# Stores of converted weights and of bias groups issued by GpSimd instead of the sync engine

## The chip, the cores and the metric

The kernel runs on one core of one Trainium2 chip. Its time is the device time of one execution in microseconds (us); the kernel before took 1183.42 us in the median of three runs (1183.03 to 1185.1). The engines are named as the profile names them: PE is TensorE, DVE is VectorE, ACT is ScalarE, POOL is GpSimd, SP is the sync engine. "PEld" is the loading of weights into TensorE, "SPq" and "DVEq" are the instruction queues of an engine. A DMA is a transfer between the chip's memory (HBM) and the core's on-chip memory (SBUF); it is started by an instruction of SP or another engine and moved by the core's 16 DMA engines.

## The reference

Attention with a learned bias, then two gated feed-forward blocks, all in float32. Cut to what matters:

```python
# B, H, S, D = 4, 8, 576, 64
psi_rel = np.log1p(np.abs(rel)); psi_i = np.log1p(np.maximum(pos[:, None], 1.0))
x = (psi_rel / psi_i)[..., None]
h = np.maximum(x @ w1 + b1, 0.0)                 # 32 hidden values for each pair (i, j)
bias = h @ w2                                    # one value for each head and pair
scores = (q @ k^T) / np.sqrt(D) + bias.transpose(2, 0, 1)[None]
attn = exp(scores - max); attn = attn / (sum(attn) + 1e-9)
x = (attn @ v), heads laid side by side: 2304 tokens x 512
x = (sigmoid(x @ w_gate) * (x @ w_val)) @ w_out                      # d_ff 1536
h = x @ w_in;  out = (h * clip(h + 3, 0, 6) / 6) @ w_out2            # d_ff 2048
```

The weights of the feed-forward blocks are handed over as float64; the bias does not depend on the batch.

## The kernel before, in words

The 576 query positions are cut into five chunks (128, 128, 128, 128 and 64 positions for all four batches). A chunk goes through attention first, in 16 units (4 pairs of heads times 4 batches; 8 units for the last chunk), and then through 68 feed-forward steps (`STEPS`, line 51), each a product of a 512 x 128 block of weights with up to 512 tokens. `moe_step` (line 430) runs one step; `product` (line 403) makes each product of three passes, high part times high part, high times low, low times high, so 12 matmuls of 512 columns a step.

The program has a lead and five blocks. The lead (lines 481 to 523) makes the bias of the first chunk and its attention. Block k (lines 622 to 634) runs the 68 steps of chunk k and, between them, the bias and the attention of a later chunk.

**The bias.** It is made in groups of 16 positions, 36 in all. `bias_hidden` (line 117) makes the hidden values `z` on ACT and DVE, `bias_mm` (line 130) multiplies by the second weight matrix on PE, `bias_out` (line 140) brings the group from PSUM to the tile `bo` (three buffers, line 72) on DVE or ACT (lines 147 and 149) and stores it to `biasD[c]` in HBM, 288 KB a group (line 153). `bias_read` (line 161) loads the stored bias of two heads as `bm`, 576 KB. Groups 0 to 7 are the first chunk's; the lead also makes groups 8 to 10.

**The weights.** In block 0 only, `w_load` loads a step's weights as float64 bits (`wd`, 512 KB, line 370; three buffers), and `w_split` (lines 376 to 398) turns them into two float32r parts in `wp` (six buffers): ACT makes `cm` (line 385), DVE works on it three times (lines 386, 387, 390), ACT writes the high part (line 395), DVE the low part (line 396). The result is used by the step's product and stored to `wsp` in HBM, 512 KB (line 397). From block 1 on a step loads its `wp` from `wsp` (line 374).

**The order.** In the lead the order on PE, ACT, DVE and SP is that of the source (line 484). After it the order of PE alone is written out; a scheduler puts DVE, ACT, SP and POOL in an order by its own estimate of times. Every engine runs its instructions in order, and a DMA-issuing instruction holds its queue until what it waits for is there. All transfers are issued by SP; POOL only sets four constants.

The lines around the two stores:

```python
        i0 = 16 * G - QC[c][0]
        nc.sync.dma_start(out=biasD[c][i0:i0 + 16].rearrange("i h j -> (i h) j"), in_=bo)      # L153
...
        nc.scalar.activation(out=wv[:, 0], in_=f, func=AF.Copy)                                # L395
        nc.vector.tensor_tensor(out=wv[:, 1], in0=f, in1=wv[:, 0].bitcast(F32), op=ALU.subtract)
        nc.sync.dma_start(out=wsp[n], in_=wv.bitcast(F32))                                     # L397
```

Of the kernel before, what the change touches and what calls it, by code (L numbers as in the profile page):

```python
# [9 lines left out]
F32 = mybir.dt.float32  # L10
# [46 lines left out]
def fused_kernel(ctx: ExitStack, tc: tile.TileContext, qd, kd, vd, tz, rd, zc, w2b, iden, wpack, out):  # L57
    nc = tc.nc
# [27 lines left out]
    biasD = [dr_p.tile([n, H, S], F32, name=f"biasD{c}") for c, (_, n) in enumerate(QC)]  # L86
    wsp = dr_p.tile([NSTEP, 128, 2, 512], F32, name="wsp")
# [17 lines left out]
    for g in (2, 3):  # L105
        nc.tensor.matmul(
            out=ps[32 * g:32 * g + 32, 0:2], lhsT=w2b_t, rhs=zc_t[:, 0:2], start=True, stop=True,
# [32 lines left out]
    def bias_out(G):  # L140

        ps = bo_q.pop(G)
        c = min(G // 8, NC - 1)
        bo = bo_p.tile([128, S], F32, name="bo")
        bv = bo.rearrange("p (a j) -> p a j", a=2)
        if c == 1:
            nc.scalar.activation(out=bv, in_=ps[:, :, 0:NI], func=AF.Identity, scale=D ** 0.5, bias=cv_t)
        else:
            nc.vector.tensor_scalar(
                out=bv, in0=ps[:, :, 0:NI], scalar1=D ** 0.5, scalar2=cv_t, op0=ALU.mult, op1=ALU.add  # L150
            )
        i0 = 16 * G - QC[c][0]
        nc.sync.dma_start(out=biasD[c][i0:i0 + 16].rearrange("i h j -> (i h) j"), in_=bo)  # L153

# [220 lines left out]
    def w_split(n):  # L377

        if n >= NSTEP:
            return  # L380
        wd = wf_q.pop(n)
        low, high = wd[:, :, 0], wd[:, :, 1]
        m = A["cv"].tile([128, 512], U32, name="cm")
        f = m.bitcast(F32)
        nc.scalar.activation(out=f, in_=high.bitcast(F32), func=AF.Copy, scale=2.0 ** -112)  # L385
        nc.vector.tensor_scalar(out=m, in0=m, scalar1=3, scalar2=None, op0=ALU.logical_shift_left)
        nc.vector.scalar_tensor_tensor(  # L387
            out=m, in0=low, scalar=29, in1=m, op0=ALU.logical_shift_right, op1=ALU.bitwise_or
        )
        nc.vector.scalar_tensor_tensor(  # L390
            out=m, in0=high, scalar=0x80000000, in1=m, op0=ALU.bitwise_and, op1=ALU.bitwise_or
        )
        wp = w_p.tile([128, 2, 4, 128], F32R, name="wp")
        wv = wp.rearrange("p s c m -> p s (c m)")
        nc.scalar.activation(out=wv[:, 0], in_=f, func=AF.Copy)  # L395
        nc.vector.tensor_tensor(out=wv[:, 1], in0=f, in1=wv[:, 0].bitcast(F32), op=ALU.subtract)  # L396
        nc.sync.dma_start(out=wsp[n], in_=wv.bitcast(F32))  # L397
        wq[n] = wp


# [80 lines left out]
    with ExitStack() as lead:  # L481
# [9 lines left out]
        for G in range(NG0 + NG1 + 1):  # L491
            if G < NG0 + NG1:
                for g in range(4):
                    bias_hidden(G, g)
                bias_mm(G)
            if G:
                bias_out(G - 1)
            if G == NG0:
                bias_read(us[0])
# [3 lines left out]
        for n in range(NL + 2):  # L503
            if n + 3 < NL:
                att_load(us[n + 3])
            if n < NL:
                att_exp(us[n])
            if n + 1 < NL:
                att_min(us[n + 1])
            if 1 <= n <= NL:  # L510
                for part in range(3):
                    att_tr(us[n - 1], part, mm_ps)
            if n < NL:
                att_norm(us[n])
            if n >= 2:
                att_av(us[n - 2], mm_ps)
                att_x(us[n - 2])
            if n + 2 < NL:
                att_qk(us[n + 2])
            if n >= NL:  # L520
                w_split(n - NL)
            if n == NL - 4:
                gate = issued[0]
# [13 lines left out]
    def chunk_bias(c, t0, dt, done=0):  # L537

        i0, n = QC[c]
        G0, nG = i0 // 16 + done, n // 16 - done  # L540
        ev = []
        for g in range(nG):
            ev.append((t0 + dt * g, lambda G=G0 + g: [bias_hidden(G, t) for t in range(4)]))
        for g in range(0, nG, 2):
            def outs(G=G0 + g, two=min(2, nG - g)):
                for i in range(two):
                    bias_mm(G + i)
                for i in range(two):
                    bias_out(G + i)
            ev.append((t0 + dt * g + dt + 1, outs))  # L550
        return ev
# [69 lines left out]
    with tc.manual_schedule(engines={ET.PE}):  # L621
        for k in range(NC):
            if k == 1:
                conv.close()
                A.update(ks=late("ks", 2), qs=late("qs", 2))
            ev = block_events(k)
            for i in range(NSTEP):
                while ev and ev[0][0] <= i:
                    ev.pop(0)[1]()
                w_load(k * NSTEP + i + WA)  # L630
                w_split(k * NSTEP + i + WB)
                moe_step(k, i, P, mm_ps)
            for e in ev:
                e[1]()
# [64 lines left out]
```

## Time and profile before

| what | value |
|---|---|
| median of three runs | 1183.42 us (1183.03 to 1185.1) |
| profiled execution: time, span of its profile | 1183.61 us, 1181.8 us |
| PE busy | 1157.1 us (98%) |
| DVE, ACT busy | 641.1 us (54%), 563.9 us (48%) |
| POOL busy | 0.2 us |
| mean DMA rate | 252 GB/s, one queue |
| bias stores, stores of converted weights | 36 of 288 KB, 68 of 512 KB |

The 1.8 us between the time and the span lie outside what the profile shows. An engine's busy time is the union of its instructions; PE's ends are modelled, so a busy PE is not PE at its peak. In the list of transfers "us to landing" is the time from the issue to the arrival of all data. In the chain of waits each piece is what held the end of the program at that time.

### The profile page before, as it was taken

The page shows a single profiled execution, that of the slowest core. Times are in us where ns is not written, and L with a number is a line of the kernel's source. Part 1 is how long each engine was busy: PE and PEld are TensorE (multiplying, and loading weights), DVE is VectorE, ACT ScalarE, POOL GpSimd, SP SyncE. Part 2 cuts the span into 40 slices and gives each one's busy share as a digit, 9 for nine tenths or more (in the row PEclk, how much of TensorE's full clock was granted, in tenths as well). Part 3 has the DMA queues.
Part 4 walks back from the last instruction along what each step waited for, and adds up shares of the span by engine and source line. Part 5 has one row for each costly group of instructions (what it writes and reads, how often), then busy time and mean ns, then how long its engine had stood idle before and what let it go on. Part 6 is the DMA issues. An engine that isn't in the chain of part 4 may idle for free.

```text
span 1181.8 us, 20334 instructions
## 1 busy us (share of the span) xinstructions
PE 1157.1 (98%) x7676; PEld 928.3 (79%) x7676; DVE 641.1 (54%) x1524; ACT 563.9 (48%) x1133; POOL 0.2 (0%) x4
## 2 busy tenths in 40 slices
PE   7998989999999999999999999999999999999998
PEld 3676767777777787777888787888878778789998
DVE  6787988999973544585534543453432315331232
ACT  7776766677752434575534543454322214331231
POOL 0000000000000000000000000000000000000000
PEclk9899999999999999999999999999999999999999
DMA  6886899999987676566575656565685857567997
GB/s 217 283 281 215 306 340 353 368 353 321 380 271 239 209 231 223 196 223 214 207 245 190 228 187 219 196 205 190 197 268 194 261 190 238 192 194 249 361 366 273
DMA packets 115264, 297.65 MB, mean 252 GB/s; under 512 B 20448, under 2 KB 35168, under 8 KB 115168
## 3 DMA queue, kind: packets, MB, share of 16 engines
q1 hardware_dynamic: 115168, 296.36, 73.1%
q8 instruction: 61, 1.00, 0.3%
q14 instruction: 35, 0.29, 0.1%
HBM read 245.32 MB, written 50.99 MB: 251 GB/s over the span
## 4 chain that ended last, share of the span: by engine, by line
PE 87%; DMA 5%; DVE 5%; ACT 2%; issue 1%; SPq 0%; ACTq 0%; DVEq 0%
PE ps L412 66%; PE ps L279 6%; PE ps L260 6%; DMA wd<-wpack 3%; PE ps L320 3%; PE ps L135 3%; PE ps L212 2%; DMA biasD<-bo 1%; DVE cm L390 1%; DVE cm L387 1%; PE ps L326 1%; DVE wp L396 1%; ACT s L237 1%; DVE s L227 1%; ACT cm L385 0%
## 5 line engine op out<-in xcount | busy, mean ns | idle before, releaser
L412 PE MATMUL ps<-xyh,wp 128*128 128x512 f32 (+1 forms) x1600 | 479.2, 375 | 6.9 <-ACT wp L395 3.5
L412 PEld LDWEIGHTS ps<-xyh,wp 128*128 128x128 f32 x1600 | 290.9, 189 | 70.7 <-issue 7.2
L412 PE MATMUL ps<-gh,wp 128*128 128x512 f32 (+1 forms) x1120 | 343.7, 378 | 0.0
L412 PE MATMUL ps<-xyl,wp 128*128 128x512 f32 (+1 forms) x800 | 295.9, 370 | 0.7 <-DVE xyl L425 0.7
L412 PEld LDWEIGHTS ps<-gh,wp 128*128 128x128 f32 x1120 | 203.5, 189 | 40.9 <-issue 6.4
L412 PE MATMUL ps<-gl,wp 128*128 128x512 f32 (+1 forms) x560 | 206.8, 369 | 0.0
L412 PEld LDWEIGHTS ps<-xyl,wp 128*128 128x128 f32 x800 | 151.5, 189 | 23.7 <-DVE xyl L425 1.1
L263 ACT ACTIVATE pT<-ps 128x384 f32<-128x384 f32 x216 | 100.6, 488 | 125.3 <-PE ps L260 124.7
L421 ACT ACTIVATE gh<-tmp 128x512 fp32r<-128x512 f32 (+1 forms) x140 | 82.4, 589 | 111.6 <-DVE tmp L443 73.7
L423 DVE TENSOR_TENSOR gl<-tmp,gh 128x512 fp32r<-128x512 f32 (+1 forms) x140 | 89.0, 636 | 65.1 <-ACT gh L421 65.1
L237 ACT ACTIVATE s<-s,m 128x576 f32<-128x576 f32 x144 | 110.4, 769 | 25.6 <-DVE m L342 13.4
L412 PEld LDWEIGHTS ps<-gl,wp 128*128 128x128 f32 x560 | 105.9, 189 | 14.9
L260 PE MATMUL ps<-id_t,s 128*128 128x128 f32 x648 | 101.1, 277 | 0.9 <-ACT s L237 0.4
L260 PEld LDWEIGHTS ps<-id_t,s 128*128 128x128 f32 x648 | 79.0, 141 | 29.0 <-issue 5.9
L443 DVE SCALAR_TENSOR_TENSOR tmp<-tmp,ps 128x512 f32<-128x512 f32 (+1 forms) x60 | 38.0, 633 | 115.2 <-PE ps L412 115.2
L279 PE MATMUL ps<-pT,vt 128*64 128x128 f32 (+1 forms) x1600 | 90.9, 266 | 0.3 <-DVE xyl L299 0.3
L279 PEld LDWEIGHTS ps<-pT,vt 128*64 128x64 f32 x1600 | 78.9, 137 | 15.0 <-issue 11.0
L449 DVE SCALAR_TENSOR_TENSOR tmp<-tmp,ps 128x512 f32<-128x512 f32 (+1 forms) x80 | 50.5, 631 | 70.4 <-ACT tmp L448 68.8
L247 DVE TENSOR_SCALAR s<-s,r 128x576 f32<-128x576 f32 x144 | 68.2, 516 | 1.6
L439 ACT ACTIVATE tmp<-ps 128x512 f32<-128x512 f32 (+1 forms) x60 | 33.3, 554 | 73.6 <-PE ps L412 73.6
L448 ACT ACTIVATE tmp<-ps 128x512 f32<-128x512 f32 (+1 forms) x80 | 44.1, 551 | 46.8 <-PE ps L412 46.0
L299 DVE TENSOR_TENSOR xyl<-ps,xyh 128x128 fp32r<-128x128 f32 (+1 forms) x52 | 17.7, 340 | 87.2 <-ACT xyh L298 87.1
(50 smaller groups left out, 939.5 us busy)
## 6 DMA issues: line engine op xcount, KB each, us to landing
wp<-wsp SPq DMA_DIRECT2D x272, 512.0 KB, 4.0
wd<-wpack SPq DMA_DIRECT2D x68, 512.0 KB, 5.5
wsp<-wp SPq DMA_DIRECT2D x68, 512.0 KB, 4.9
vt<-vd SPq DMA_DIRECT2D x80, 320.0 KB, 4.5
kt<-kd SPq DMA_DIRECT2D x80, 288.0 KB, 5.1
biasD<-bo SPq DMA_DIRECT2D x36, 288.0 KB, 2.8
bm<-biasD SPq DMA_DIRECT2D x16, 576.0 KB, 5.0
qt<-qd SPq DMA_DIRECT2D x16, 256.0 KB, 6.4
```

The lines of the kernel that those rows point to most:

```text
L135: nc.tensor.matmul(out=ps[32 * g:32 * g + 32, j, 0:NI], lhsT=w2b_t, rhs=z[:, g, NI * j:NI * j + NI], start=True, stop=True, tile_position= ...
L237: nc.scalar.activation(out=s[:, h], in_=s[:, h], func=AF.Exp, scale=-1.0, bias=d["m"][:, h:h + 1], accum_out=r[:, h:h + 1],)
L247: nc.vector.tensor_scalar(out=s[:, h], in0=s[:, h], scalar1=r[:, h:h + 1], scalar2=None, op0=ALU.mult)
L260: nc.tensor.transpose(out=ps[:, t * NQ:t * NQ + NQ], in_=p[:, 128 * k:128 * k + 128], identity=id_t)
L263: nc.scalar.activation(out=d["pt"][:, 3 * part:3 * part + 3], in_=ps[:, 0:3 * NQ].rearrange("p (t n) -> p t n", t=3), func=AF.Copy,)
L279: nc.tensor.matmul(out=po[64 * h:64 * h + 64, n * a:n * a + n], lhsT=vt[:, v], rhs=pt[:, k, n * a:n * a + n], start=(t == 0), stop=(t == 4 ...
L412: nc.tensor.matmul(out=ps[:, 0:nt], lhsT=w[:, c, :], rhs=x[:, 0:nt], start=(first and c == 0 and i == 0), stop=(last and c == 3 and i == 2),)
L421: nc.scalar.activation(out=hi[:, 0:nt], in_=src, func=AF.Copy, scale=scale)
L423: nc.vector.tensor_tensor(out=lo[:, 0:nt], in0=src, in1=hi[:, 0:nt].bitcast(F32), op=ALU.subtract)
L443: nc.vector.scalar_tensor_tensor(out=th, in0=th, scalar=1.0, in1=ps, op0=ALU.add, op1=ALU.mult)
L448: nc.scalar.activation(out=t, in_=ps, func=AF.Relu, bias=3.0)
L449: nc.vector.scalar_tensor_tensor(out=t, in0=t, scalar=6.0, in1=ps, op0=ALU.min, op1=ALU.mult)
```

## The change

Both stores are issued by GpSimd's queue. Every load, and the stores of the output, stay with SP.

```diff
@@ bias_out
         i0 = 16 * G - QC[c][0]
-        nc.sync.dma_start(out=biasD[c][i0:i0 + 16].rearrange("i h j -> (i h) j"), in_=bo)
+        nc.gpsimd.dma_start(out=biasD[c][i0:i0 + 16].rearrange("i h j -> (i h) j"), in_=bo)
@@ w_split
         nc.vector.tensor_tensor(out=wv[:, 1], in0=f, in1=wv[:, 0].bitcast(F32), op=ALU.subtract)
-        nc.sync.dma_start(out=wsp[n], in_=wv.bitcast(F32))
+        nc.gpsimd.dma_start(out=wsp[n], in_=wv.bitcast(F32))
         wq[n] = wp
```

SP's list of the lead before, from the last load of the start on (the first eight bias stores are like the two shown):

```order
L490 DMA tz_t_96<-tz 128x448
L153 DMA biasD0_90<-bo_178 128x576
...
L153 DMA biasD0_90<-bo_297 128x576
L167 DMA bm_300<-biasD0_90 128x1152
L153 DMA biasD1_91<-bo_316 128x576
...
L153 DMA biasD1_91<-bo_336 128x576
L182 DMA kt_356<-kd 128x576
```

SP's list of the same place now, and below it POOL's list of the whole lead:

```order
L490 DMA tz_t_96<-tz 128x448
L167 DMA bm_300<-biasD0_90 128x1152
L182 DMA kt_356<-kd 128x576
L185 DMA vt_358<-vd 128x640
L167 DMA bm_377<-biasD0_90 128x1152
```

```order
L694 UNCONDITIONAL_BRANCH
L153 DMA biasD0_90<-bo_178 128x576
...
L153 DMA biasD0_90<-bo_297 128x576
L153 DMA biasD1_91<-bo_316 128x576
...
L153 DMA biasD1_91<-bo_336 128x576
L397 DMA wsp_95<-wp_1139 128x1024
```

The eleven stores of the lead left SP for POOL and kept their order among themselves; the load of `bm` now waits for stores of another queue.

In block 0, DVE's list before, around the first attention unit of the second chunk (`L227` adds the bias and takes the minimum, `L386`, `L387`, `L390` and `L396` convert weights, `wd_1650` is the load of one step, `wp_1712` its result):

```order
L387 SCALAR_TENSOR_TENSOR cm_1707<-wd_1650,cm_1707 128x512
L386 TENSOR_SCALAR cm_1757<-cm_1757 128x512
L390 SCALAR_TENSOR_TENSOR cm_1707<-wd_1650,cm_1707 128x512
L227 ISA s_1744,m_1745<-ps_1738,bm_1642 128x576
...
L423 TENSOR_TENSOR gl_1731<-tmp_1703,gh_1730 128x512
L387 SCALAR_TENSOR_TENSOR cm_1757<-wd_1679,cm_1757 128x512
L227 ISA s_1744,m_1745<-ps_1739,bm_1642 128x576
...
L396 TENSOR_TENSOR wp_1712<-cm_1707,wp_1712 128x512
```

The same place of DVE's list now:

```order
L387 SCALAR_TENSOR_TENSOR cm_1707<-wd_1650,cm_1707 128x512
L227 ISA s_1744,m_1745<-ps_1738,bm_1642 128x576
...
L423 TENSOR_TENSOR gl_1731<-tmp_1703,gh_1730 128x512
L227 ISA s_1744,m_1745<-ps_1739,bm_1642 128x576
...
L390 SCALAR_TENSOR_TENSOR cm_1707<-wd_1650,cm_1707 128x512
L386 TENSOR_SCALAR cm_1757<-cm_1757 128x512
...
L387 SCALAR_TENSOR_TENSOR cm_1757<-wd_1679,cm_1757 128x512
...
L390 SCALAR_TENSOR_TENSOR cm_1757<-wd_1679,cm_1757 128x512
L247 TENSOR_SCALAR s_1744<-s_1744,r_1746 128x576 x2
L396 TENSOR_TENSOR wp_1712<-cm_1707,wp_1712 128x512
```

The conversion of `wp_1712` now has the unit's softmax (`L227` to `L247`) and most of the next conversion ahead of its last step. PE's list is the same in both programs.

## Rows read from the trace of the kernel before

**Rows 1.** Busy time by stretch; columns: stretch, length, engines, TensorE clock, DMA share, GB/s.

```profile
99.25:237.72 138.47, 133.28 (x732) 100.86 (x732) 126.25 (x254) 92.67 (x174) 0.00 (x0) 0.99 0.92 334
237.72:1181.80 944.08, 939.77 (x6172) 770.55 (x6172) 444.11 (x1080) 397.50 (x800) 0.00 (x0) 1.00 0.71 241
```

**Rows 2.** What PE waited for from 238 us to the end.

```profile
PE ps L412 <- DVE xyl L425: 0.7, 1, 0.7
```

**Rows 3.** The chain of waits in the lead: start, length, what.

```profile
12.92 5.09 DMA biasD<-bo
...
19.97 3.23 DMA biasD<-bo
...
25.14 2.07 DMA biasD<-bo
...
27.35 4.59 DMA bm<-biasD
...
32.09 0.76 DVE s L227
```

**Rows 4.** Order of time in the lead on SP: start, length, what.

```profile
10.55 0.33 SPq L490 DMA_DIRECT2D tz_t<-tz  x1
11.45 14.00 SPq L153 DMA_DIRECT2D biasD<-bo  x8
```

**Rows 5.** The first bias store, alone in its window; then the DMA rate from 10 to 18 us.

```profile
DMA to landing us min/median/max: 5.9/5.9/5.9
...
GB/s 397 402 392 439 394 422 389 420 405 416 402 415 396 376 394 402 393 393 408 405 396 393 416 422 389 387 421 402 384 410 421 288 161 81 69 58 46 58 23 23
```

**Rows 6.** Order of time in the lead on DVE; in brackets idle time before, and its releaser.

```profile
14.52 1.06 DVE L126 TENSOR_SCALAR z<-tz_t,sc_t,zc_t 128x576 f32<-128x576 f32 x2
17.42 0.82 DVE L149 TENSOR_SCALAR bo<-ps,cv_t 128x576 f32<-128x576 f32 x1 [1.85 <-DMA biasD<-bo]
...
24.30 0.81 DVE L149 TENSOR_SCALAR bo<-ps,cv_t 128x576 f32<-128x576 f32 x1
25.03 2.04 DVE L126 TENSOR_SCALAR z<-tz_t,sc_t,zc_t 128x576 f32<-128x576 f32 x4
```

**Rows 7.** Order of time in the lead on PE.

```profile
7.24 9.55 PE L135 MATMUL ps<-z,w2b_t 128*32 128x288 f32 x80 [1.73 <-ACT z L124]
18.39 10.72 PE L135 MATMUL ps<-z,w2b_t 128*32 128x288 f32 x96 [1.60 <-DVE bo L149]
...
30.71 1.23 PE L212 MATMUL ps<-kt,qt 64*128 64x288 f32 x6 [0.92 <-ACT bo L147]
```

**Rows 8.** What SP's queue waited for, 99 to 238 us: total, times, longest.

```profile
SPq L370 <- DVE cm L390: 30.5, 25, 2.8
```

**Rows 9.** The chain of waits in block 0: the first and last of five loads.

```profile
145.17 8.14 DMA wd<-wpack
...
196.28 8.51 DMA wd<-wpack
```

**Rows 10.** PE in block 0: the costliest group, then two of its gaps in order of time.

```profile
L412 PE MATMUL ps<-xyh,wp 128*128 128x512 f32 x199 | 66.4, 405 | 6.9 <-ACT wp L395 3.5 <-DVE wp L396 3.4
...
99.25 0.50 PE L412 MATMUL ps<-xyh,wp 128*128 128x512 f32 x1 [2.43 <-ACT wp L395]
141.48 0.73 PE L412 MATMUL ps<-xyh,wp 128*128 128x512 f32 x2 [0.81 <-DVE wp L396]
```

**Rows 11.** Waits of ACT for loaded weights, 99 to 238 us.

```profile
ACT cm L385 <- DMA wd<-wpack: 9.6, 8, 2.8
```

**Rows 12.** Stores of `wp` in 99.25 to 237.72 us: issues, then landing.

```profile
L397 SPq DMA_DIRECT2D wsp<-wp x40: 319/326/1152, 99.9 to 236.5; - x40
...
DMA to landing us min/median/max: 2.6/5.3/10.0
```

**Rows 13.** Two DVE pieces of the chain in block 0.

```profile
169.44 0.60 DVE cm L387
...
171.63 0.93 DVE s L247 x2
```

## The prediction

> **What bounds the kernel now.** I read the busy time by stretch first [rows 1]. From 237.72 us to the end PE is busy 939.77 of 944.08 us and waits in all 0.7 us for another engine [rows 2]; whatever the change does, it can only be paid or earned in the 238 us before. There are two stages there. One is the lead, up to 99.25 us, which the chain below explains. In the other, the first part of block 0 (99.25 to 237.72), PE is busy 133.28 of 138.47 us, DVE 126.25, and the DMA engines 0.92 of the time: three resources near their end at once. After 237.72 PE alone sets the pace.
>
> The chain of waits says what the lead hangs on [rows 3]: a bias store of 5.09 us, one of 3.23, the last one of the chunk, 2.07, and then the load of `bm`, 4.59, which lets the first attention unit start at 32.09. So the latency of bias stores is on the path. In block 0 the chain runs through five loads of `wd`, the first at 145.17 and the last at 196.28 us [rows 9], with conversions on DVE between them.
>
> **The change part by part. SP's issue time.** 104 issues leave SP (36 and 68). That gives nothing by itself: in block 0 SP's waits before a `wd` load are for `cm` L390, 25 times, 30.5 us [rows 8]. L390 is the last reader of the load's own buffer, and three buffers are all there are; a load that stands behind no store would wait for the same buffer. Term: 0. If that cover went, the price would be SP's 0.33 us an issue [rows 4].
>
> **The first stores of the lead: −1.6 us.** The first bias store is issued at 11.45, right behind the opening loads in one queue (the last of them at 10.55) [rows 4], and lands after 5.9 us, while the DMA engines move about 400 GB/s until 16 us [rows 5]. `bo` has three buffers, so the fourth group waits for that landing: DVE stands 1.85 us until 17.42, with its two `z` done at 15.57 [rows 6], and PE stands 1.60 us until 18.39 [rows 7]. From POOL the store does not stand behind those loads. I give it the 3.23 us of the store at 19.97 [rows 3] plus 1.16 for POOL (next paragraph): 11.0 + 4.39 = 15.4, before 15.57. Then the stall is gone, and PE's 1.60 is what the rest of the bias gains, since PE has no other gap up to 29 us. The loads that are overtaken are needed at about 29 us; the overtaking bytes (three times 288 KB at 400 GB/s, 2.2 us) leave them more than 10 us.
>
> **POOL's extra latency on the last store: +1.16 us.** No transfer of POOL is in the trace. From below: nothing is gained on the last store, which found its queue drained and landed in 2.07, so 0. From above: the slowest bias store of the chain of waits, 5.09, less 2.07, that is 3.0. I take 3.23 − 2.07 = 1.16, the spread between two stores in a drained queue [rows 3], the nearest rows. The middle groups just bear this: from the end of one `bo` to the next use of its buffer lie three groups of 1.72 us less 0.81, 4.35 us (the fourth group at 17.42, the eighth at 24.30, four steps of 1.72 [rows 6]), against 3.23 + 1.16 = 4.39. Then the last `bo` ends at 25.11 − 1.6 = 23.5, lands at 26.7, `bm` is issued 0.14 later and lands after 4.59, and the first unit starts at 31.65 instead of 32.09. PE's side of that unit (the matmuls at 30.71 behind ACT's `bo` [rows 7]) moves up by the same 1.6 and is not late. The lead gains 0.44, and all later work of the lead hangs on that unit.
>
> **Loads of weights beside the stores: −1.2 us.** Where a store now goes out from another queue, a load issued behind it shares the DMA engines with it instead of standing behind all of it: at most half a store, 512 KB at 400 GB/s being 1.3 us, so 0.65 a load. Five loads are in the chain, 3.3 us, a third of the 9.6 us that ACT waits for `wd` [rows 11]. PE's gaps in the stage are 6.9 us in the costliest group; 2.43 of them at 99.25 and 0.81 at 141.48 come ahead of the chain's first such load [rows 10]. A third of the other 3.7 is 1.2; the ends are 0 and 3.7.
>
> **The new order on DVE: +1.5 us.** PE's list is unchanged, DVE's is not. Ahead of the last step of `wp_1712`, for which PE already waits in the old program, now stand one more conversion step, 0.60, and the two L247, 0.93 [rows 13]; the ends are 0, where the load comes that much sooner, and 3.7, where the new list loses once more what PE lost there before. Later in the block the new list is about one conversion ahead of the old one at the same product, for which I count nothing, as PE paces that part.
>
> **Cover elsewhere.** A store of `wp` may land late by the whole 10.0 us of the slowest one [rows 12]: its buffer comes round after six steps of about 3.4 us (40 stores from 99.9 to 236.5 us, in the same rows). If that cover were gone, ACT's L395 and then PE would wait for the excess. On POOL a bias store stands behind stores of weights that wait for DVE's L396; SP's next load of `bm` waits for it, and `wd` loads behind that. Before, the `wd` load behind it was late by its own buffer, so 1 to 2 us are hidden. In blocks 1 and 3 the same wait stands before loads of `wp` that run four steps ahead: 0, or 1.16 for each of three chunks without that lead.
>
> **Sum.** −1.6 + 1.16 − 1.2 + 1.5 = −0.1 us against the profiled execution, 1183.61 us (span 1181.8 and 1.8 outside it), which is 0.2 above the median of the runs. Forecast 1183.5, no change. What this kernel's measurement can tell from no change is 0.2%, 2.4 us: faster is below 1181.0, slower above 1185.8.
>
> **The rivals.** *DVE holds POOL up (slower).* DVE's `z` work (L126) stands right behind each `bo`: 1.06 us behind most, 2.04 behind the last [rows 6]. If POOL can't prepare a store while these run, the last store is late by 2.04 more, and the middle ones land after 3.23 + 1.16 + 1.06 = 5.45 instead of the 4.35 that the buffers bear, 1.1 late in two rounds of three groups: −0.1 + 2.04 + 2.2 = +4.1, 1187.7. It decides from a delay of about 0.6 us a store. For it: DVE is saturated there; 576 values in 0.5 us is faster than the 0.81 of `bo` for as many, so these are another kind of operation. Against: no row shows any such wait.
>
> The Trainium skill ("SBUF — State Buffer", in "SBUF: two separate sides") warns of this: descriptors of a GpSimd transfer are written through a port that DVE holds in its two-port modes. By it the sum would be this rival's; no run here shows it yet.
>
> *The own queue gives nothing (slower, barely).* If the DMA engines, full until 16 us [rows 5], serve the first store no earlier than now, it lands at 17.36 + 1.16 and the stall grows by 1.16 instead of going: 1.16 + 1.16 − 1.2 + 1.5 = +2.6, 1186.2. For it: 400 GB/s has no slack. Against: work in another queue need not wait for the end of the first.
>
> The Trainium skill ("DMA: Bandwidth & Descriptors", "Issuing engines are not separate DMA queues") says that issuing from several engines saves only the issuer's time; by that the first stores and the loads of weights would gain nothing, and the sum would be 1.16 + 1.16 + 1.5 = +3.8.
>
> *POOL is slower than a group (slower).* Eight stores come 1.72 us apart. If POOL takes 2.7 us for each, the last is seven times 1.0 late: 1190. Nothing in the trace bears on it.
>
> *The loads were the whole loss (faster).* If the 3.7 us of PE's gaps go, and the order costs nothing: −0.44 − 3.7 = −4.1, 1179.5. For it: five `wd` loads in one chain. Against: DVE is busy 126.25 of 138.47 us there, so little of it is DVE's to give.
>
> **How the numbers follow.** Forecast 0.45 (its own range 1181 to 1186: 0.41 no change, 0.03 faster, 0.01 slower); DVE holds POOL up 0.20 (0.17 slower, 0.03 no change); own queue gives nothing 0.11 (0.07 slower, 0.04 no change); POOL slower than a group 0.06, slower; the loads were the whole loss 0.18, faster. Together faster 0.21, no change 0.48, slower 0.31. From 1179 to 1188 us lies all but the case of the slow POOL (0.06) and the far ends of its neighbours and of the faster case (about 0.1).
>
> **What would show it.** The first step: DVE's `bo` at 17.42 starts near 15.6 with no idle time on a store. The second: the last store of the first chunk takes about 3.2 us to land, and the first L227 starts near 31.7. The third: loads of `wd` between 145 and 205 us land about 0.65 us sooner, and PE's gaps in the L412 group sum to 5 to 7.5 us. From then on PE's pace is the same. I am wrong if the stall in the lead stays, if bias stores take over 4.4 us, if DVE's rows L126, L247 or L386 grow longer than now, or if POOL's queue has stores waiting for POOL itself.

## The result, and the profile after

The changed kernel took 1192.07 us in the median (1191.01 to 1193.99, four runs), the kernel before 1183.22 us beside it (1182.87 to 1185.1): a ratio of 1.0062, with a 95% interval of 1.0047 to 1.0076. The quotient of the two medians is 1.0075; the loss is 7 to 9 us. It is slower, and lies outside the range of 1179 to 1188 us. The profiled execution (1193.99 us, the slowest of the four) has a span of 1192.2 us, 10.4 more than before. Of that 9.9 is there when block 1 begins: its first bias product (L135) starts at 384.83 us instead of 374.89, and the distance stays.

I go through the profile in the order of the prediction. First the lead, in the chain of waits (start, length, what), to be read against [rows 3]:

```profile
11.25 5.70 DMA biasD<-bo
...
17.04 0.06 DVE bo L149
...
23.27 0.80 POOL biasD L153
24.07 1.01 issue
25.10 3.51 DMA biasD<-bo
...
28.75 4.53 DMA bm<-biasD
...
33.42 0.76 DVE s L227
```

The first store still takes 5.70 us (5.9 in [rows 5]), so DVE's wait for it at 17.04 only shrank, from 1.85 us to the 1.52 below. The last `bo` ends at 24.68 (before: 25.11), but `bm` is issued at 28.75 instead of 27.35. From the end of the last `bo` to that issue it is 4.07 us instead of 2.24. POOL's and DVE's order of time (start, length, instruction, in brackets the idle time before it) show a part of the reason:

```profile
23.27 0.80 POOL L153 DMA_DIRECT2D biasD<-bo  x1 [0.90 <-DVE bo L149]
25.10 2.20 POOL L153 DMA_DIRECT2D biasD<-bo  x2 [1.03 <-DVE bo L149]
28.48 0.54 POOL L153 DMA_DIRECT2D biasD<-bo  x1 [1.19 <-ACT bo L147]
```

DVE in the same time:

```profile
17.04 0.82 DVE L149 TENSOR_SCALAR bo<-ps,cv_t 128x576 f32<-128x576 f32 x1 [1.52 <-DMA biasD<-bo]
...
22.89 1.06 DVE L126 TENSOR_SCALAR z<-tz_t,sc_t,zc_t 128x576 f32<-128x576 f32 x2
23.87 0.81 DVE L149 TENSOR_SCALAR bo<-ps,cv_t 128x576 f32<-128x576 f32 x1
24.60 2.04 DVE L126 TENSOR_SCALAR z<-tz_t,sc_t,zc_t 128x576 f32<-128x576 f32 x4
```

The store that POOL begins at 23.27, while DVE makes two `z` (L126), takes 0.80 us and is done 0.12 us after the second of them (24.07 against 23.95). The store at 25.10 begins beside four `z`, takes 1.67 us and is done 0.13 us after the fourth (26.77 against 26.64; the x2 row holds that store and the next, 0.54). Stores that begin with no `z` under way take 0.54. In e9 (below) the same store beside four `z` took 0.69 us, from 25.08, and was done 0.13 us after the second of them, so 1.67 is no fixed price. The Trainium skill ("SBUF — State Buffer", "SBUF: two separate sides") has the two engines exclude each other at a shared port; these rows agree in kind.

In block 0 the changed kernel is ahead at first: the first attention unit (L212) starts at 151.10 instead of 152.13. Then PE stands. Its order of time in the kernel after, to be set beside the same two waits of the kernel before:

```profile
151.10 1.24 PE L212 MATMUL ps<-kt,qt 64*128 64x288 f32 x8
160.71 0.80 PE L412 MATMUL ps<-xyh,wp 128*128 128x512 f32 x1 [5.42 <-ACT wp L395]
162.70 1.22 PE L412 MATMUL ps<-xyh,wp 128*128 128x512 f32 x2 [0.76 <-DVE wp L396]
```

PE in the kernel before:

```profile
157.37 0.50 PE L412 MATMUL ps<-xyh,wp 128*128 128x512 f32 x1 [1.05 <-ACT wp L395]
159.86 0.73 PE L412 MATMUL ps<-xyh,wp 128*128 128x512 f32 x2 [1.76 <-DVE wp L396]
```

After the long wait the granted clock falls to the lower of TensorE's two levels (1.2 GHz), where before it stayed at 1.00. Busy time by stretch of the kernel after (columns as in [rows 1]):

```profile
155.00:160.00 5.00, 0.29 (x2) 0.00 (x0) 4.32 (x11) 3.69 (x8) 0.00 (x0) 0.87 0.61 247
160.00:165.00 5.00, 3.52 (x7) 2.33 (x8) 4.79 (x10) 2.58 (x5) 1.06 (x2) 0.50 0.80 268
```

The second unit starts at 171.1 instead of 165.5. Behind PE's waits stands a load of `wd`, seen in ACT's order of time and in the chain, where it answers to the first of [rows 9] (8.14 us):

```profile
154.95 0.66 ACT L385 ACTIVATE cm<-wd 128x512 f32<-128x512 f32 x1 [4.02 <-DMA wd<-wpack]
```

The load itself, in the chain of waits:

```profile
143.81 11.06 DMA wd<-wpack
```

It lands at 154.87, 1.56 us later than that load of the kernel before (153.31). From there to the second of PE's two starts above it is 7.83 us (162.70) instead of 6.55 (159.86): in DVE's new list the softmax and the next conversion come ahead. So PE is 2.84 us late there, by the load and by the order; the rest of the 5.6 us builds up at the lower clock.

The list of transfers of 142 to 156 us says why the load takes 11 us (columns of the last three rows: what, queue, count, size of one, median us to landing):

```profile
q1 hardware_dynamic: 822, 3.13, 63.1%
q0 software_dynamic: 583, 2.13, 37.5%
...
wsp<-wp POOLq DMA_DIRECT2D x4, 512.0 KB, 7.5
wd<-wpack SPq DMA_DIRECT2D x3, 512.0 KB, 11.1
bm<-biasD SPq DMA_DIRECT2D x2, 576.0 KB, 7.9
```

Two loads of `bm` stand in front of the load in SP's queue (q1), and 2.13 of the 5.26 MB that move meanwhile are POOL's stores (q0). In the kernel before the median load of `wd` in this stretch landed after 8.3 us, and the store after 8.6. It is not the number of stores, of which that kernel issued five in the stretch, nor are POOL's bytes dearer: 2.13 MB took 37.5% of the engines' time, SP's 3.13 MB 63.1%. What differs is their place. The load and a store that POOL issues 2 us behind it, in order of time, and then that store's time to landing:

```profile
143.81 6.86 SPq L370 DMA_DIRECT2D wd<-wpack  x3
145.82 0.53 POOL L397 DMA_DIRECT2D wsp<-wp  x1 [2.94 <-DVE wp L396]
DMA to landing us min/median/max: 8.4/8.4/8.4
```

The store lands at 154.2, ahead of the load. In the kernel before, as far as the profile tells, none of SP's 115 transfers from 99 to 262 us landed ahead of one that was issued earlier.

Two views show that this was not the end of it. After 238 us PE waits for four things, 3.6 us in all, where [rows 2] had one of 0.7:

```profile
PE ps L412 <- ACT xyh L421: 1.5, 1, 1.5
PE ps L412 <- DVE xyl L425: 0.9, 1, 0.9
PE ps L412 <- DVE tmp L449: 0.6, 1, 0.6
PE ps L279 <- ACT pT L263: 0.6, 1, 0.6
```

And DVE is busy 121.95 us in the first stretch of [rows 1], where it was 126.25:

```profile
99.25:237.72 138.47, 132.03 (x716) 100.69 (x717) 121.95 (x244) 89.38 (x167) 24.17 (x44) 0.95 0.91 325
```

### The profile page after: what moved, and what is told of

It reads as the page before. It is cut to its first block, busy times and chain, and to the rows that moved or that the text cites. A ratio compares the mean times of both kernels' runs of the same rounds, so it can differ in the third digit from the quotient of the medians.

```text
span 1192.2 us, 20398 instructions
## 1 busy us (share of the span) xinstructions
PE 1161.6 (97%) x7676; PEld 931.7 (78%) x7676; DVE 642.0 (54%) x1524; ACT 563.2 (47%) x1133; POOL 62.7 (5%) x108
## 4 chain that ended last, share of the span: by engine, by line
PE 82%; DVE 8%; DMA 5%; ACT 3%; issue 2%; SPq 0%; POOL 0%; DVEq 0%; ACTq 0%; POOLq 0%
PE ps L412 63%; PE ps L279 6%; PE ps L260 5%; DMA wd<-wpack 4%; PE ps L320 3%; PE ps L135 2%; PE ps L212 2%; DVE cm L387 2%; DVE cm L390 1%; DVE wp L396 1%; DVE s L227 1%; ACT cm L385 1%; DMA biasD<-bo 1%; ACT s L237 1%; PE ps L326 1%
## 5 line engine op out<-in xcount | busy, mean ns | idle before, releaser
L412 PE MATMUL ps<-xyh,wp 128*128 128x512 f32 (+1 forms) x1600 | 481.8, 377 | 10.8 <-ACT wp L395 7.9
L412 PEld LDWEIGHTS ps<-xyh,wp 128*128 128x128 f32 x1600 | 292.7, 190 | 74.9 <-ACT wp L395 8.5
L412 PE MATMUL ps<-gh,wp 128*128 128x512 f32 (+1 forms) x1120 | 343.8, 378 | 0.0
L412 PE MATMUL ps<-xyl,wp 128*128 128x512 f32 (+1 forms) x800 | 297.4, 372 | 0.9 <-DVE xyl L425 0.9
L412 PEld LDWEIGHTS ps<-gh,wp 128*128 128x128 f32 x1120 | 203.5, 189 | 41.1 <-issue 7.0
L412 PE MATMUL ps<-gl,wp 128*128 128x512 f32 (+1 forms) x560 | 206.8, 369 | 0.0
L412 PEld LDWEIGHTS ps<-xyl,wp 128*128 128x128 f32 x800 | 152.5, 191 | 24.1 <-DVE xyl L425 1.2
L421 ACT ACTIVATE gh<-tmp 128x512 fp32r<-128x512 f32 (+1 forms) x140 | 82.4, 589 | 113.0 <-DVE tmp L443 73.0
L412 PEld LDWEIGHTS ps<-gl,wp 128*128 128x128 f32 x560 | 105.9, 189 | 14.9
L247 DVE TENSOR_SCALAR s<-s,r 128x576 f32<-128x576 f32 x144 | 68.2, 516 | 1.7
```

What stands on the lines that cost most here:

```text
L247: nc.vector.tensor_scalar(out=s[:, h], in0=s[:, h], scalar1=r[:, h:h + 1], scalar2=None, op0=ALU.mult)
L412: nc.tensor.matmul(out=ps[:, 0:nt], lhsT=w[:, c, :], rhs=x[:, 0:nt], start=(first and c == 0 and i == 0), stop=(last and c == 3 and i == 2),)
L421: nc.scalar.activation(out=hi[:, 0:nt], in_=src, func=AF.Copy, scale=scale)
```

## The experiments

The ratios below are to runs of the kernel before on the same chip; "us by the ratio" is the ratio's excess times 1184 us. A profile shows one execution, and 23 executions of the kernel before on one chip took 1180.3 to 1190.5 us, so a difference of 2 us between two profiles says little by itself. At the start there were three theories. A: stores from POOL's queue take turns with loads on the DMA engines, so one load is late and PE runs dry. B: the scheduler's new order of DVE and ACT is the loss. C: late bias stores hold up SP's queue.

**One half of the change alone** (e1: L153 from POOL, e2: L397 from POOL; everything scheduled anew).

> Only the 36 bias stores go to POOL; the stores of converted weights stay on SP. Theory A (POOL's stores of weights share the DMA engines with the loads of wd, one load lands late, PE runs dry near 155 us and its clock falls): few such stores are left, so no gap above 2.5 us on PE between 140 and 250 us, and 1183 to 1185 us. Theory B (the new order on DVE makes wp late, whatever the queue): the order is changed here too, so 1186 to 1192 us with a PE gap on wp of 3 us or more. Theory C (bias stores land later from POOL and hold SP's loads behind bm): as slow as the changed kernel, 1190 to 1193 us.

> Only the 68 stores of converted weights go to POOL; the bias stores stay on SP. Theory A: the load of wd behind the two bm still lands after 10 us or more, PE stands 4 us or more near 155 us, 1189 to 1193 us. Theory B: the order differs from both kernels, anything from 1182 to 1192 us. Theory C: as before, 1182 to 1185 us.

e1 took 1190.96 us, ratio 1.0056 (1.0035 to 1.0076); e2 1191.35 us, 1.0051 (1.0031 to 1.0070). e2's time is where A had it, and e1's where B and C had it. The signs in the profiles failed: PE's waits near 157 us are 1.34 and 1.77 us in e2, not 4, and the longest in e1 is 2.55, not 3. That each half costs nearly as much as the whole no theory had foreseen. C is out (e2 should have been as before). DVE's and ACT's order differs from the kernel before in both runs, so each changes two things, and A and B are not told apart.

**Source order after the lead, with both queues** (e5 stores from SP, e6 from POOL).

```diff
-    with tc.manual_schedule(engines={ET.PE}):
+    with tc.manual_schedule(engines={ET.PE, ET.Activation, ET.DVE}):
```

> The kernel before with DVE and ACT in the order of the source after the lead too (the scheduler orders SP alone). A base for its partner with the same edit and both stores on POOL; the orders of PE, DVE and ACT are the same in the two. No theory gives its own time; estimate 1183 to 1215 us.

> The changed kernel with DVE and ACT in the order of the source after the lead too: PE, DVE and ACT stand in the same order as in its partner, only the stores' queue differs. Theory A: 3 to 10 us slower than the partner, with loads of wd landing later in 140 to 250 us. Theory B: within 2.4 us of the partner. Theory C: 3 to 10 us slower, with the loss beginning where SP waits for a bias store.

1290.6 and 1293.02 us, ratios 1.0903 (1.0882 to 1.0925) and 1.0923 (1.0899 to 1.0948): 2.4 us between the medians, under A's 3 and within the intervals, in a kernel that is 9% slower. It is inconclusive for the tuned one.

**Orders held.** From here on a table of instruction numbers, taken from a scheduled kernel, fixes the order on DVE, ACT, SP and POOL, by edges that set the order alone and add no wait:

```diff
+    fix_order(tc)
+def fix_order(tc):
+    traced = {i.name: i for i in tc.nc.cur_bb.bb.instructions}
+    for code in ORDERS:
...
+            now = traced[f"I-{at}"]
...
+                tc.add_manual_dep(
+                    now, last.name, mybir.DependencyInfo(mybir.DependencyClass.NoSync, mybir.DependencyReason.DATA),
+                    reason="fix_order",
+                )
```

e7 has the stores on POOL and the order of the kernel before, e8 the stores on SP and the order of the changed kernel.

> The stores go out from POOL as in the changed kernel, but DVE, ACT and SP's loads are held to the order that the kernel before has. Theory A (the stores from POOL take turns with the loads on the DMA engines; the load of wd behind the two loads of bm lands late, PE runs dry near 155 us and its granted clock falls): 1188 to 1193 us, that load lands after 10 us or more, PE waits 4 us or more near 155 to 163 us. Theory B (the loss is the new order that the scheduler gives DVE and ACT): 1182 to 1186 us, and the waits there are those of the kernel before, 2 to 3 us in sum, with the clock at 1.00. About 1187 would mean a part of each.

> The stores go out from SP as in the kernel before, but DVE and ACT, and the loads on SP among themselves, are held to the order that the changed kernel has. Theory A (the stores' own queue is the cause): 1182 to 1186 us, the load of wd behind the two of bm lands after 8 to 9 us. Theory B (the order is the cause): 1188 to 1193 us with PE's waits near 155 us of 4 us or more.

e7: 1190.87 us, 1.0052 (1.0037 to 1.0066), 6.2 us by the ratio. e8: 1188.87 us, 1.0032 (1.0018 to 1.0046), 3.8 us. So both A and B hold in part; by the ratio their sum, 10.0, is more than the 7.3 of the change (8.9 by the medians), about as far as the intervals reach. e8 shows how an order that is ahead can lose: its first unit starts at 148.2 us, 3.9 earlier than before, and then ACT waits for the load behind the two of `bm` just as in the changed kernel, with no store on POOL:

```profile
150.90 0.66 ACT L385 ACTIVATE cm<-wd 128x512 f32<-128x512 f32 x1 [3.76 <-DMA wd<-wpack]
```

The load in the chain of waits of e8, and the second of PE's two starts behind it:

```profile
140.98 9.84 DMA wd<-wpack
158.65 1.22 PE L412 MATMUL ps<-xyh,wp 128*128 128x512 f32 x2 [0.77 <-DVE wp L396]
```

From the landing (150.82) to that start it is 7.83 us, as in the changed kernel.

In e7 A's numbers for that place were missed: PE's waits there are 1.50 and 1.77 us, not 4, and the load lands after 7.3 us, not 10. Its loss is spread: the first product is 1.0 us later, the first unit 2.3, the last one 5.4.

**Each half, at the old order** (e9 bias stores on POOL, e10 stores of weights on POOL).

> Only the bias stores go out from POOL; DVE, ACT and SP are held to the order of the kernel before. If the queue's price of 6 us (e7) is the sum of its two halves: the lead's part here, the first product about 1.0 us later (as in e7, 100.25 instead of 99.25), 1185 to 1187 us. If either half alone costs all of it (a threshold): 1189 to 1192 us.

> Only the stores of converted weights go out from POOL; DVE, ACT and SP are held to the order of the kernel before. Sum of halves: the greater part, 1187 to 1190 us, the load of wd behind the loads of bm lands after 9 us or more, and waits for wd on ACT up to 240 us grow from 9.6 to 12 us or more. If it is the bias stores that matter: 1183 to 1186 us.

e9: 1187.69 us, 1.0024 (1.0012 to 1.0037). e10: 1188.69 us, 1.0025 (1.0013 to 1.0038). Once the order is held the halves add up to e7 (0.49% and 0.52%). In e9's profile the first product starts at 97.90 us, not at the 100.25 that was expected; ten profiles with bias stores on SP have it between 96.65 and 99.25 us, and that of the kernel before is the latest of them. In e10 ACT's waits for `wd`, 99 to 262 us (total, times, longest), are longer than those of the kernel before, which has the row of [rows 11] in this stretch too; DVE's waits for ACT's `cm` grow from 6.3 to 10.1 us, and the median load of `wd` lands after 5.7 us instead of 5.3.

```profile
ACT cm L385 <- DMA wd<-wpack: 15.6, 12, 2.9
```

**PE's wait filled** (e11; the changed kernel, held to its own order).

```diff
         ps = ps_q[0]
+        if n == 17:
+            for i in range(22):
+                nc.tensor.matmul(
+                    out=ps[:, 0:nt], lhsT=fill[0][:, 0, i % 4, :], rhs=ops[i % 4][0][:, 0:nt], start=True, stop=True
+                )
+        fill[0] = wp
```

> The changed kernel, all engines held to its own order, with 22 more matmuls of 512 columns (5.1 us at 2.4 GHz) put where PE stood 5.42 us before step 17; their result is overwritten. Theory C (of the 6.6 us lost there 3 are the granted clock that falls to 0.50 behind the wait): the clock stays at 1.00 from 155 to 172 us, the second unit starts 2 to 3 us behind the kernel before instead of 5.6, and the time is 1187 to 1190 us. Rival (the clock costs nothing, since DVE or the loads pace that stretch anyway): the second unit starts as late as in the changed kernel, 1191 to 1194 us.

1192.4 us, 1.0062 (1.0047 to 1.0077): no change to the changed kernel. Yet the clock did what theory C of that run said. Busy time by stretch comes first, then PE's order of time (L411 is the filling, L418 and L427 are L412 and L421 of the other kernels):

```profile
155.00:160.00 5.00, 5.00 (x24) 4.14 (x23) 4.96 (x13) 3.41 (x8) 0.00 (x0) 1.00 0.72 275
160.00:165.00 5.00, 4.58 (x21) 3.47 (x20) 4.75 (x10) 2.54 (x4) 1.06 (x2) 1.00 0.85 313
```

PE's order of time:

```profile
155.66 5.15 PE L411 MATMUL ps<-xyh,wp 128*128 128x512 f32 x22
...
204.60 0.87 PE L279 MATMUL ps<-pT,vt 128*64 128x128 f32 x10 [1.53 <-ACT pT L263]
218.32 0.87 PE L279 MATMUL ps<-pT,vt 128*64 128x128 f32 x10 [1.27 <-ACT pT L263]
243.05 0.49 PE L418 MATMUL ps<-xyh,wp 128*128 128x512 f32 x1 [1.75 <-ACT xyh L427]
```

The second unit starts 1.7 us behind the kernel before (5.6 without the filling), the sixth 4.7, the eighth 7.7. What PE got back at 165 us it lost again by 245 us to ACT and DVE; ACT waits 21.4 us for `wd`, 14.0 without the filling. PE's wait and its clock are how the loss looks at 160 us; they don't set the end.

**What sets it.** The profiles side by side, in the order of the second column (the last unit is the 16th L212 of block 0; e12, e15 and e4 come below):

| kernel | DVE busy, 99 to 262 us | ACT waits for `wd` there | last unit starts |
|---|---|---|---|
| e11 (wait filled) | 144.49 | 21.4 | 345.2 |
| changed | 144.66 | 14.0 | 346.1 |
| e7 (POOL, old order) | 145.84 | 13.8 | 341.6 |
| e10 (weights on POOL, old order) | 146.15 | 15.6 | 340.4 |
| e9 (bias on POOL, old order) | 149.13 | 9.7 | 337.8 |
| e8 (SP, new order) | 149.42 | 10.0 | 338.4 |
| before | 150.14 | 9.6 | 336.2 |
| e12 (POOL, four buffers) | 151.40 | 5.5 | 337.5 |
| e15 (SP, four buffers, old order) | 151.77 | 6.9 | 334.1 |
| e4 (SP, four buffers) | 156.47 | 3.3 | 331.4 |

The less DVE has done by 262 us, the later the last unit, with only small steps out of line. As DVE has the same work to do in all ten, the column shows the delay as DVE sees it, and not yet a cause. That gave theory D: late loads leave DVE idle, and DVE has no slack in block 0 to make it up.

**DVE given slack** (e16 on POOL, e17 on SP, both at the old order).

```diff
-        for h in range(2):
+        for h in range(0 if u[0] == 1 else 2):
             nc.vector.tensor_scalar(
                 out=s[:, h], in0=s[:, h], scalar1=r[:, h:h + 1], scalar2=None, op0=ALU.mult
```

> As e7 (stores from POOL, the order of the kernel before), but the second chunk's 32 multiplications by 1/sum (L247, 0.51 us each, 16.5 us of DVE between 157 and 345 us) are left out, so that its attention is not normalised. Theory D (DVE has no slack in block 0, so every late load stays lost): with that slack only what is lost ahead of 160 us is left, the lead's 1 to 1.5 us and the wait behind the loads of bm, so this run is 1 to 4 us above e17 instead of the 6.2 that e7 costs. Rival (the loads pace the block whatever DVE does): 5 to 8 us above e17.

> The kernel before in its own order, with the same 32 multiplications left out. Theory D: 1177 to 1182 us, since the 2.8 us of PE's waits near 157 us come ahead of most of that slack and little else is lost. Rival: 1183 to 1186 us.

e17: 1182.27 us, 0.9974 (0.9960 to 0.9987); e16: 1186.1 us, 1.0013 (0.9999 to 1.0028). They lie 3.8 us apart by the medians and 4.6 by the ratios: between D's upper end, 4, and the rival's 5. As each ratio is known to about 1.6 us, 4.6 can't be told from e7's 6.2 either. In the profiles e16 is 0.6 us behind its partner e17 at the second unit and 2.9 at the last, as e7 went from 4.3 to 5.4 against the kernel before: slack on DVE did not end the loss behind 165 us. ACT's waits for `wd` grew (16.8 us and 15.0): DVE then frees the buffers sooner, and the loads are next. D is not shown. DVE and the loads are both near their end in block 0.

**Half the bytes** (e13 on POOL, e14 on SP, at the old order; L397 stores 64 partitions, and L374 reads them twice).

> As e10 (stores of converted weights from POOL, the order of the kernel before on DVE, ACT and SP), but each such store writes 64 of the 128 partitions, 256 KB instead of 512; later loads read those twice, so half of the weights of blocks 1 to 4 are not the right ones. Theory S (stores issued later take turns on the DMA engines with loads that are already under way): with half the bytes the price of the own queue, this run less e14, falls from 3.0 to 1.5 us or less, and ACT's waits for wd up to 262 us fall from 15.6 to under 11 us. Rival E (it is GpSimd's way of issuing, whatever the bytes): this run stays 2.5 to 4 us above e14, and ACT's waits for wd 5 us or more above e14's.

> The kernel before, in its own order, with the same half stores issued by SP (half of the weights of blocks 1 to 4 are not the right ones). Theory S: with fewer bytes in front of them the loads of wd land sooner, 1179 to 1183 us. Rival (loads are paced by their buffers alone): 1183 to 1186 us.

Their whole times, 3240.41 and 3235.13 us, tell nothing of the stores, since the later loads became slow in this form (last section); only block 0 can be compared. ACT's waits for `wd` are put at 3.9 and 4.1 us, but in e13 a wait of ACT that is put down to DVE also ended when a load had landed. First the load in the chain of waits, then ACT's order of time:

```profile
144.36 8.94 DMA wd<-wpack
153.38 0.67 ACT L385 ACTIVATE cm<-wd 128x512 f32<-128x512 f32 x1 [1.14 <-DVE tmp L443]
```

All of ACT's waits at L385 but those for L396, from 99 to 262 us, are 6.1 us in e13 and 4.1 in e14; in e10 and the kernel before they are 17.4 and 12.0. With half the bytes 2.0 us are left of 5.4, as S says, where E had 5 or more. The last unit starts at 334.5 and 331.6 us, still 2.9 apart where e10 and the kernel before were 4.2, which is nearer to E. So the late loads go with the bytes of the stores, which supports turns on the DMA engines as their cause; as these engines are also less busy in both runs (0.83 and 0.86 of that time, 0.93 before), it does not prove it. What else POOL's queue costs in e13 is open.

**A fourth buffer for `wd`** (e3 the changed kernel, e4 the kernel before, both scheduled anew; e12 stores on POOL at e4's order; e15 the kernel before at its own order).

```diff
-    for name, bufs in (("wf", 3), ("cv", 2)):
+    for name, bufs in (("wf", 4), ("cv", 2)):
```

> The changed kernel with four buffers for loaded weights (wd) instead of three. Theory A: loads are issued a step, some 3.4 us, earlier, so the late one near 145 us is hidden; PE's wait near 155 us falls under 3 us, the clock stays at 1.00 there, 1181 to 1186 us. Theory B: a further buffer doesn't undo an order that is worse: 1187 to 1192 us.

> The kernel before with four buffers for loaded weights instead of three; the scheduler orders DVE, ACT and SP anew. Theory A: the 2.8 us of PE's waits at 157 and 160 us shrink or go, 1179 to 1184 us. Theory B (any new order costs): 1186 to 1191 us.

> Four buffers for loaded weights, stores from POOL, and DVE, ACT and SP's loads held to the order of e4. Theory A (the stores in their own queue take the DMA engines' time from the loads, which four buffers hide in part): 1181 to 1185 us, as e3. Rival (the remaining 4.8 us between e3 and e4 are the order): 1177 to 1180 us, as e4.

> The kernel before with four buffers for loaded weights, all engines held to its own order. If the buffer is what makes e4 faster: 1177 to 1181 us. If it is e4's new order: 1182 to 1185 us.

e3: 1183.64 us, 0.9994 (0.9981 to 1.0007). e4: 1178.83 us, 0.9948 (0.9931 to 0.9965). e12: 1185.07 us, 0.9995 (0.9979 to 1.0011). e15: 1181.09 us, 0.9956 (0.9940 to 0.9972). The buffer gives 0.4 to 0.5% with SP's stores, at either order, and takes the whole loss off the changed kernel. The queue still costs 0.47% at four buffers and one order (e12 against e4). e4 is faster than both kernels.

## Why the prediction was wrong

The step that failed is "Loads of weights beside the stores: −1.2". It saw only what a load gains when no earlier store stands before it. It left out that stores issued later, which nobody waits for, no longer stand behind the load but move beside it, as the one at 145.82 us did. With the weights' stores alone on POOL and the order unchanged the price is 3.0 us by the ratio (e10), ACT's waits for `wd` 15.6 instead of 9.6 us: 4 us off, and of the wrong sign.

- "SP's issue time: 0" held. SP's loads of `wd` now wait for `cm` L390 37 times, 116.7 us up to 238 us; [rows 8] had 25 times, 30.5. Without stores between, it stands at the buffer at once.
- "The first stores of the lead: −1.6" failed: 0.33 of the 1.85 us. The rival "own queue gives nothing" had this right: with the DMA engines full until 16 us [rows 5], a queue of its own did not land this store sooner. It was wrong that the stall would grow.
- "POOL's extra latency on the last store: +1.16" measured +1.83, inside its bounds. Of that 1.13 is POOL's own 1.67 against 0.54 beside DVE's four `z`, so "DVE holds POOL up" is real, in this profile at about half of the 2.04 that it gave the last store; the middle stores lose 0.26 each, under its point of 0.6, and wait for nothing.
- Together the lead was to gain 0.44. The first L227 starts at 33.1 us in the mean of nine kernels with bias stores on POOL (32.19 to 33.74; the changed one, e1, e3, e6, e7, e9, e11, e12, e16) and at 31.9 in that of ten with them on SP (31.28 to 32.25; before, e2, e4, e5, e8, e10, e13, e14, e15, e17): a loss of 1.2. One profile of each would not have shown that, as these spread by 1 us.
- "The new order on DVE: +1.5" is 3.8 us (e8), at the upper bound of 3.7. At the place named, ahead of the last step of `wp_1712`, it came near: 1.28 us, 7.83 instead of 6.55 from the load's landing. What it left out are the loads behind `bm`, which the new order reaches sooner and must wait for longer: in e8 the first unit is 3.9 us ahead, the load after it only 2.5.
- "Cover elsewhere: 0" held: stores of `wp` land after 11.0 us at the latest, [rows 12] 10.0, and from block 1 on the distance stays.
- Of the signs of being wrong, the stall that stays and the bias stores of over 4.4 us came (5.70). DVE's rows did not grow: L126 takes 573 ns in the mean (572 before), L247 516 (516), L386 424 (420).
- The premise that everything must be paid before 238 us was wrong. PE's 0.7 us of waits [rows 2] said nothing on DVE, which in the kernel before was busy 23.63 of the 24 us from 238 to 262. The delay reached PE through ACT and DVE at 242, 320 and 329 us.
- The Trainium skill ("DMA: Bandwidth & Descriptors", "Issuing engines are not separate DMA queues") says that transfers of all issuers run on the same engines and interleave. The two queues' shares above agree. I had read from it that nothing is gained; that a load loses its place ahead of later stores is what e10 adds.

Slower came, to which the prediction gave 0.31 against 0.48 for no change. Where the lead, the loads and the order stood at −0.44, −1.2 and +1.5, e9 (all 36 bias stores), e10 and e8 give 2.8, 3.0 and 3.8 us; their sum, 9.6, is near the 7 to 9 of the change. The range failed because no case had the loads' term as a loss, and because it left out the costly ends falling together: +1.16 for a stall that grows, +3.0 for the last store, 0 for the loads and +3.7 for the order give 1191.5.

## What to carry to other kernels

SP's queue kept its transfers in order, and so gave a load its place ahead of every later store; before moving stores nobody waits for to a queue of their own, ask which urgent loads they will then share the DMA engines with, and how many buffers those loads have. Where three resources are near their end, price a change by what it takes from each, not by the waits of the one that ends last: filling PE's wait and restoring its clock gave nothing. And an edit that lets a scheduler run again changes two things; hold the order before reading halves.

## What was not expected of the hardware

- A GpSimd-issued store of 288 KB held POOL 0.54 us alone. Begun while DVE made `z` in the lead, it ended 0.12 to 0.13 us after one of them did, 0.69 to 1.67 us from its start.
- A wait of PE of 5.42 us was followed by a granted clock of 0.50 from 160 to 165 us; with 22 matmuls in the wait it stayed at 1.00.
- In e13 a load of 512 KB whose source is 64 partitions read twice moved at about 52 GB/s, with the 16 DMA engines busy 0.13 of the time from 1030 to 1060 us; the DMA rate from 1000 to 1100 us, 40 slices:

```profile
GB/s 52 52 100 237 127 52 151 53 47 52 52 52 52 63 52 52 52 52 52 52 52 52 52 52 52 54 52 52 98 72 75 223 197 43 66 326 132 52 52 74
```
